# The first unit of K, loaded as eight transfers of every eighth partition, the first of them ahead of all weights

## The chip, the cores and the metric

The kernel runs on one core of a Trainium2 chip. The core has five engines that run their own instruction streams: TensorE (PE in the profile; PEld is its loading of weights), VectorE (DVE), ScalarE (ACT), GpSimd (POOL) and SyncE (SP), which here does nothing but issue transfers. Sixteen DMA engines carry data between HBM and the on-chip memory SBUF, which has 128 partitions. The metric is the device time of one execution in microseconds (us), as a median over runs.

## The reference

Two branches start from the same normalized input and are added to it. Branch A is one decoding step of attention with a cached window, branch B a small mixer and MLP. There are 4 sequences (B), one token each, width 576; attention has 32 query heads on 16 key/value heads (G = 16) of width 128, and the last 2048 of 8192 cached positions are read.

```python
def _A_ref(x, k_cache, v_cache, wq, wo):
    W = min(4096, max(256, Sk // 4))
    q = (x @ wq).reshape(B, Sq, Hq, Dh).transpose(0, 2, 1, 3)
    k = jnp.repeat(k_cache[:, :, Sk - W:, :], rep, axis=1)
    v = jnp.repeat(v_cache[:, :, Sk - W:, :], rep, axis=1)
    scores = jnp.einsum("bhqd,bhkd->bhqk", q, k) * (Dh ** -0.5)
    p = _softmax(scores, axis=-1)
    o = jnp.einsum("bhqk,bhkd->bhqd", p, v)
    return o.transpose(0, 2, 1, 3).reshape(B, Sq, Hq * Dh) @ wo

def _B_ref(x, w1, w2, w3, w4):
    h = _gelu(_layernorm(x, axis=-1) @ w1)
    ...
    x1 = x + hs
    return x1 + _gelu(_layernorm(x1, axis=-1) @ w3) @ w4

xn = _layernorm(A_x, axis=-1)
return A_x + _A_ref(xn, ...) + _B_ref(xn, ...)
```

With one token per sequence, the shifts of branch B (left out above) leave nothing of the shifted parts.

## The kernel before

The work is small in arithmetic and large in data: 88.5 MB of caches and weights pass through SBUF once. The kernel builds a list of operations for each engine. `add` (line 168) puts one on an engine's list with what it waits for, the signal that it gives and a key; `add_dma` (line 172) does the same for one or several transfers, which share a semaphore that grows by 16 for each. At the end every list is sorted by key (line 564), and that is the engine's program. So the order on SP's queue is the order of keys, and an operation that waits holds up all that stands behind it on its engine.

On SP's queue stand, in this order: `wq` in three transfers (keys -20, -18, -15; lines 221 to 223), W1 and W2 of branch B with two each (-14, -13), W3 in three (-12, -10, -8), then the units of K (keys 0 to 15) with the first unit of V between (key 8.5), then the rest of V, `wo` and W4 in five pieces. The small input x is issued by ScalarE at the very start.

A unit (`kv_pairs`, line 231) is one key/value head for all four sequences: 128 partitions of 16 KB, 2 MB in one transfer. Partition p = 4i + b holds 64 consecutive positions of sequence b, for i from 0 to 31. K's units go to a ring of four slots (`kring`), V's to another (`vring`), so from the fifth on a K unit waits for the last transposes of the unit four before it.

TensorE's order: the projections of the weights as they land, zeroing of the score accumulators (`pe_zeroS`, key -1, line 326), and then a loop of four rounds of four units. For each unit it transposes K in eight groups of eight blocks (`pe_T`, line 337), which DVE and ScalarE copy out of PSUM, and multiplies the transposed K with the queries (line 353). The first transposes of each unit wait for that unit's semaphore, ("k", slot), to reach 16 in each round. Then come the softmax, the products with V (line 434), `wo` and W4 (lines 449 and 531), and the output.

## Time and profile before

| | us |
|---|---|
| median of 3 runs | 215.08 |
| lowest and highest | 215.01, 215.12 |
| the profiled execution, device time | 215.35 |
| its span, first to last instruction | 214.0 |

| engine | busy us | share of the span |
|---|---|---|
| PE | 139.3 | 65% |
| PEld | 108.2 | 51% |
| DVE | 85.1 | 40% |
| ACT | 59.3 | 28% |
| POOL | 10.8 | 5% |

The profile page divides the span into 40 equal slices. A row of digits gives the busy share of an engine in each, in tenths; the row "DMA" the mean busy share of the 16 DMA engines, and "GB/s" what they moved. A row of the windows gives, for a stretch of time that begins the row, its length, the busy time and number of instructions of PE, PEld, DVE, ACT and POOL, then the clock granted to TensorE, the DMA share (1.00 is 16 engines busy) and GB/s; a packet is counted where it starts, so a short window can show a share above 1. Rows of queues give the packets that start in the window, their MB, and the time that they take as a share of 16 engines over the window. A row of the chain of waits gives start, duration, and what the end of the program hung on in that time. Rows of DMA packets count all and those under 512 B, which are almost all the 4-byte marks with which an engine reports its part of a transfer done.

### The profile page before, as it was taken

The page shows a single profiled execution, that of the slowest core. Times are in us where ns is not written, and L with a number is a line of the kernel's source. Part 1 is how long each engine was busy: PE and PEld are TensorE (multiplying, and loading weights), DVE is VectorE, ACT ScalarE, POOL GpSimd, SP SyncE. Part 2 cuts the span into 40 slices and gives each one's busy share as a digit, 9 for nine tenths or more (in the row PEclk, how much of TensorE's full clock was granted, in tenths as well). Part 3 has the DMA queues.
Part 4 walks back from the last instruction along what each step waited for, and adds up shares of the span by engine and source line. Part 5 has one row for each costly group of instructions (what it writes and reads, how often), then busy time and mean ns, then how long its engine had stood idle before and what let it go on. Part 6 is the DMA issues. An engine that isn't in the chain of part 4 may idle for free.

```text
span 214.0 us, 5789 instructions
## 1 busy us (share of the span) xinstructions
PE 139.3 (65%) x2670; PEld 108.2 (51%) x2672; DVE 85.1 (40%) x162; ACT 59.3 (28%) x72; POOL 10.8 (5%) x38
## 2 busy tenths in 40 slices
PE   0368375999999994999999719913344443333585
PEld 0114222877777883788887604813333443333444
DVE  5502602666666664466666569611111111100000
ACT  2001222466665553265666653000000000000000
POOL 8201000000000000000000000000000000000000
PEclk9999855899999999699999995555555555555579
DMA  7999999999999999999999999999999999999992
GB/s 243 426 398 447 441 405 435 416 424 426 432 423 429 429 432 426 429 429 430 426 429 429 432 429 441 423 423 426 426 432 429 423 429 426 429 432 425 428 408 108
DMA packets 6946, 88.63 MB, mean 414 GB/s; under 512 B 781, under 2 KB 1177, under 8 KB 1945
## 3 DMA queue, kind: packets, MB, share of 16 engines
q1 hardware_dynamic: 6920, 88.50, 97.7%
q8 instruction: 7, 0.11, 0.2%
q14 instruction: 3, 0.02, 0.0%
q10 hardware_dynamic: 16, 0.01, 0.0%
HBM read 88.49 MB, written 0.00 MB: 414 GB/s over the span
## 4 chain that ended last, share of the span: by engine, by line
DMA 52%; PE 36%; DVE 4%; SPq 4%; issue 2%; ACT 0%
DMA vring<-in_A_v_cache_dram 23%; PE ps L337 23%; DMA kring<-in_A_k_cache_dram 21%; DMA vring<-in_B_w_dram 8%; PE ps L353 7%; PE ps L434 4%; SPq L179 4%; PE ps L531 1%; DVE PTb L387 1%; DVE rmax L379 1%; DVE regB L345 1%; DVE PTs L395 1%; PE ps L410 0%; ACT P_sb L384 0%; DVE out_sb L558 0%
## 5 line engine op out<-in xcount | busy, mean ns | idle before, releaser
L345 DVE COPY regB<-ps 128x1024 bf16<-128x1024 bf16 x80 | 52.4, 687 | 34.3 <-PE ps L337 32.5
L337 PEld LDWEIGHTS ps<-perm_k,kring 128*128 128x128 bf16 x1024 | 58.9, 99 | 11.9 <-issue 8.6
L337 PE MATMUL ps<-perm_k,kring 128*128 128x128 bf16 x1024 | 62.2, 222 | 3.5 <-DMA kring<-in_A_k_cache_dram 3.5
L344 ACT ACTIVATE regB<-ps 128x1024 bf16<-128x1024 bf16 x48 | 47.6, 1022 | 41.1 <-PE ps L337 41.1
L434 PE MATMUL ps<-PTg,vring 128*128 128x8 bf16 x1024 | 29.5, 168 | 39.4 <-DMA vring<-in_A_v_cache_dram 37.0
L434 PEld LDWEIGHTS ps<-PTg,vring 128*128 128x128 bf16 x1024 | 28.4, 104 | 40.4 <-DMA vring<-in_A_v_cache_dram 27.5
L442 DVE TENSOR_TENSOR PTb<-ps,PTb 128x32 bf16<-128x32 f32 x16 | 3.1, 191 | 56.5 <-PE ps L434 56.5
L353 PE MATMUL ps<-regB,Qs 128*32 128x512 bf16 x272 | 18.8, 397 | 4.6 <-issue 3.5
L541 ACT ACTIVATE P_sb<-ps 100x288 f32<-100x288 f32 x1 | 0.4, 410 | 75.8 <-PE ps L449 75.8
L353 PEld LDWEIGHTS ps<-regB,Qs 128*32 128x32 bf16 x272 | 6.6, 97 | 10.8 <-issue 6.4
L398 DVE TENSOR_TENSOR PTg<-PTs,bmask 128x512 bf16<-128x512 bf16 x16 | 10.7, 681 | 0.0
L375 POOL COPY Qs<-Qpad 128x128 bf16<-128x128 bf16 x16 | 4.6, 293 | 92.6 <-PE ps L353 81.2
L515 PE MATMUL ps<-regB,x1nT 128*32 128x432 bf16 (+1 forms) x60 | 5.4, 520 | 1.9 <-DMA regB<-in_B_w_dram 1.4
L279 PE MATMUL ps<-ident_bf,xn_bf 4*128 4x4 bf16 x8 | 0.6, 170 | 8.8 <-DVE ragsrc L272 8.8
L301 PE MATMUL ps<-vring,xnT 128*32 128x512 bf16 x40 | 4.6, 629 | 2.1 <-DMA vring<-in_A_wq_dram 2.1
L388 PE MATMUL ps<-PTb,perm_p 128*128 128x512 bf16 x3 | 1.8, 609 | 4.9 <-DVE PTb L387 4.8
L279 PEld LDWEIGHTS ps<-ident_bf,xn_bf 4*128 4x128 bf16 x8 | 0.4, 112 | 8.8 <-POOL ones_f L215 6.3
L528 DVE STREAM_TRANSPOSE h2T_sb<-PTb 128x1152 bf16<-128x1152 bf16 x1 | 1.4, 1378 | 8.3 <-ACT PTb L525 8.3
L515 PEld LDWEIGHTS ps<-regB,x1nT 128*32 128x32 bf16 x60 | 2.0, 132 | 4.8 <-DMA regB<-in_B_w_dram 2.7
L558 DVE CAST out_sb<-ps 36x144 bf16<-36x144 f32 x1 | 0.3, 300 | 9.8 <-PE ps L531 9.8
L449 PE MATMUL ps<-kring,ORT 128*4 128x288 bf16 x64 | 3.8, 429 | 0.4 <-DVE ORT L463 0.4
L265 ACT ACTIVATE sd<-mv 4x1 f32<-4x1 f32 x3 | 0.6, 202 | 12.1 <-DVE mv L263 12.1
(98 smaller groups left out, 72.0 us busy)
## 6 DMA issues: line engine op xcount, KB each, us to landing
kring<-in_A_k_cache_dram SPq DMA_DIRECT2D x16, 2048.0 KB, 15.7
vring<-in_A_v_cache_dram SPq DMA_DIRECT2D x16, 2048.0 KB, 17.6
regB<-in_B_w_dram SPq DMA_DIRECT2D x2, 2304.0 KB, 21.5
kring<-in_A_wo_dram SPq DMA_DIRECT2D x1, 4608.0 KB, 24.0
vring<-in_A_wq_dram SPq DMA_DIRECT2D x2, 2048.0 KB, 9.8
vring<-in_B_w_dram SPq DMA_DIRECT2D x2, 2016.0 KB, 17.5
vring<-in_B_w_dram SPq DMA_DIRECT2D x2, 576.0 KB, 13.8
vring<-in_B_w_dram SPq DMA_DIRECT2D x1, 720.0 KB, 14.3
```

The costliest lines, as they stand in the source:

```text
L179: e.dma_start(o_, i_).then_inc(S[skey], 16)
L301: ins = e.matmul(Qps[32 * j:32 * j + 32, k, :], lhsT=x_, rhs=w, start=(r == 0), stop=(r == 4), tile_position=(0, 32 * j))
L337: ins = e.transpose(tb[n % NTB][:, t, :], kring[:, g % NKS, 8 * k + t, :], perm_k[:])
L344: return "act", lambda e: e.activation(out=ktbuf[:, n % NKT], in_=src, func=ACTF.Copy)
L345: return "dve", lambda e: e.tensor_copy(out=ktbuf[:, n % NKT], in_=src)
L353: ins = e.matmul(Sps[32 * b:32 * b + 32, c4, :].rearrange("p (t i) -> p t i", t=16), lhsT=Qs[:, g % 4, b, :], rhs=kttile[:, t0:t0 + 16, b, :],
L375: P(lambda e, g=g: e.tensor_copy(out=Qs[:, g % 4], in_=Qpad[:, g]), waits=(["qT"] if g == 0 else []) + ([f"SC{g - 4}"] if g >= 3 else []), ...
L398: add("dve", lambda e, g=g: e.tensor_tensor(out=PTg[:, g % NPG], in0=PTs[:, :, 2 * g:2 * g + 2].unsqueeze(2).to_broadcast([128, NT, B, 2]) ...
L434: ins = e.matmul(OTps(g), lhsT=vring[:, g % NVS, t, :], rhs=PTg[:, g % NPG, t].rearrange("p b e -> p (b e)"), start=(t == 0), stop=(t == N ...
L442: add("dve", lambda e, g=g: e.tensor_tensor(out=OTx[:, :, 2 * g:2 * g + 2, :], in0=OTps(g).rearrange("p (b e) -> p b e", b=B).unsqueeze(3) ...
L449: return e.matmul(ACC[h], lhsT=lhsT, rhs=rhs, start=start, stop=stop, tile_position=(k0, 32 * h))
L515: ins = e.matmul(H2ps[k][32 * j:32 * j + 32, :], lhsT=x_, rhs=w, start=(r == 0), stop=(r == 4), tile_position=(0, 32 * j))
```

## The change

The loop that issues the units of K begins with the second unit. The first is cut into eight transfers, named by s from 0 to 7. Transfer s takes the partitions s, s + 8, ..., s + 120, which are 16 partitions of 16 KB, 256 KB. Their source is sequence s mod 4 and, of the 32 stretches of positions, those with i = 2e + s // 4 for e from 0 to 15, so every partition gets the data that it had before. Transfer 0 has key -21 and stands ahead of `wq`, the first on SP's queue. Transfers 1 to 6 stand behind W3 (key -0.5), and transfer 7 (key 0) is the one that counts for the semaphore ("k", 0). Transfers 0 to 6 share a new semaphore, "comb"; TensorE waits for all seven behind the zeroing matmuls.

```diff
-        for g in range(G):
+        def comb(s_):
+            return (kring_t[s_:128:8, 0:UE],
+                    A_k_cache[s_ % B, 0, Sk - W:Sk, :].rearrange("(e j t) d -> e j (t d)", j=2, t=NT)[:, s_ // B, :])
+        add_dma([comb(0)], "comb", (), -21)
+        ev_comb = add_dma([comb(s_) for s_ in range(1, 7)], "comb", (), -0.5)
+        ev_k.append(add_dma([comb(7)], ("k", 0), (), 0))
+        add("pe", lambda e: None, [ev_comb], None, -0.5)
+        for g in range(1, G):
             ev_k.append(add_dma(kv_pairs(kring_t, g % NKS, A_k_cache, g), ("k", g % NKS),
                                 [f"T{8 * (g - NKS) + 7}"] if g >= NKS else [], g))
```

## The prediction

> **What bounds the kernel now.** I read the page from top to bottom first: the 40 slices, the queues, the chain by engine.

> ```profile
> span 214.0 us, 5789 instructions
> ...
> DMA  7999999999999999999999999999999999999992
> GB/s 243 426 398 447 441 405 435 416 424 426 432 423 429 429 432 426 429 429 430 426 429 429 432 429 441 423 423 426 426 432 429 423 429 426 429 432 425 428 408 108
> ...
> q1 hardware_dynamic: 6920, 88.50, 97.7%
> q8 instruction: 7, 0.11, 0.2%
> ```

> The 16 DMA engines are full in every slice but the first and the last two, and SP's queue (q1) carries nearly every byte. So the kernel is one stream of 88.5 MB. The windows give its speed, and how it runs out:

> ```profile
> 36.00:62.00 26.00, 24.60 (x400) 20.52 (x400) 15.70 (x25) 13.90 (x14) 1.47 (x5) 0.95 1.01 429
> 140.00:190.00 50.00, 18.10 (x621) 17.33 (x621) 7.29 (x19) 0.00 (x0) 0.00 (x0) 0.50 1.00 427
> 208.00:209.00 1.00, 0.25 (x5) 0.00 (x0) 0.00 (x0) 0.00 (x0) 0.00 (x0) 1.00 0.98 396
> 209.00:210.00 1.00, 0.97 (x32) 0.97 (x34) 0.00 (x0) 0.00 (x0) 0.00 (x0) 1.00 0.71 266
> 210.00:211.00 1.00, 1.00 (x40) 0.98 (x34) 0.00 (x0) 0.00 (x0) 0.00 (x0) 1.00 0.38 143
> 211.00:212.00 1.00, 1.00 (x32) 0.67 (x24) 0.00 (x0) 0.00 (x0) 0.00 (x0) 1.00 0.03 10
> ```

> 429 GB/s over 16 engines is 26.8 GB/s each, so a 16 KB packet (16384 B) takes 16384/26.8 = 0.611 us on its engine, and a unit of K or V (128 packets, 8 per engine) 4.89 us. The share of busy engines falls from 0.98 to 0.03 over some 2 us: the engines do not finish together, and the last one sets the end. The chain of waits says what hangs on the stream:

> ```profile
> 9.14 27.14 DMA kring<-in_A_k_cache_dram
> 36.28 0.13 issue
> 36.41 1.89 PE ps L337 x16
> ...
> 171.91 17.64 DMA vring<-in_A_v_cache_dram
> 189.55 0.05 issue
> 189.60 1.88 PE ps L434 x64
> 191.48 0.02 issue
> 191.50 17.49 DMA vring<-in_B_w_dram
> 208.99 0.04 issue
> 209.03 3.11 PE ps L531 x88
> 212.14 0.02 issue
> 212.17 0.30 DVE out_sb L558
> ```

> The V units come at the stream's pace: 17.64 + 0.05 + 1.88 + 0.02 = 19.59 us for four, 4.90 each against 4.89 of pure transfer, so the boundary between two queued transfers costs no more than about 0.01 us. The end is the landing of W4's second piece (208.99) plus 3.2 us of TensorE and DVE. Because SP's queue always holds work, **the time moves by just as much as the stream's slowest engine moves**. TensorE's long share in the K stage (L337) sits beside a full stream and buys nothing.

> **The change part by part.** *Bytes:* none are added; 256 KB of K's first unit move from behind W3 to the very front, and the other seven eighths stay at their place as seven transfers of 16 packets. *Semaphore marks:* seven more boundaries at up to 0.01 us, 0.07 us. *SP's issues:* seven more.

> ```profile
> 2.19 1.07 SPq L179 DMA_DIRECT2D vring<-in_B_w_dram  x2
> 5.42 3.68 SPq L179 DMA_DIRECT2D regB<-in_B_w_dram  x1
> 9.14 4.53 SPq L179 DMA_DIRECT2D kring<-in_A_k_cache_dram  x4
> ```

> Two issues take 1.07 us, so one is about 0.5, and seven add 3.7 us on SP; the 3.68 us of the third is SP held by a full queue, not by work. The first issue delays every weight issue by 0.5 us, the others come between W3 and K's second unit, which SP now has issued by 13.67 us and which the stream reaches after 36. That cover of over 20 us hides all of them; without it they would cost 3.7. *The new wait on PE* for the seven early eighths stands behind the zeroing matmuls and before the first transposes; behind it on PE is only T0, which waits for K's first unit anyhow. *Weights* land up to 0.61 us later; the first transposes today wait 0.45 us for K alone, so with an unmoved stream PE could start up to 0.2 us later. That moves SP's next K issues, which run far ahead: a K transfer lands 15.7 us after its issue, 4.89 of it its own. So nothing; without that lead, 0.2.

> ```profile
> 36.41 1.89 PE L337 MATMUL ps<-perm_k,kring 128*128 128x128 bf16 x16 [0.45 <-DMA kring<-in_A_k_cache_dram]
> ...
> kring<-in_A_k_cache_dram SPq DMA_DIRECT2D x16, 2048.0 KB, 15.7
> ```

> *The start.* I asked for the packets of the first microseconds by their starting times: 1.75 to 2.60, then 1.82 to 2.12, then 2.12 to 2.60.

> ```profile
> q1 hardware_dynamic: 16, 0.26, 147.3%
> ...
> q1 hardware_dynamic: 12, 0.20, 329.6%
> ...
> q1 hardware_dynamic: 4, 0.07, 54.8%
> ```

> The first packet of each engine takes 1.473 x 16 x 0.85 us / 16 = 1.25 us on average, twice the steady 0.611, and four engines start up to some 0.5 us after the other twelve. If the wait is for the 128 descriptors of the first transfer, 16 descriptors shorten it: the gain is at most the excess, 0.6 us. If it is the first reading itself, the gain is 0.

> *Where the eighths land.* The trace of before holds no transfer that touches every eighth partition. The nearest row is that of x, the only transfer to a few partitions early on: 4 packets of 1152 B into partitions 0 to 3, starting between 1.74 and 1.82. Beside it, W4's last packets of the same size, spread over 128 partitions, one engine still at work (211.04 to 211.34, seven of them and one mark).

> ```profile
> q10 hardware_dynamic: 4, 0.00, 30.9%
> ...
> q1 hardware_dynamic: 8, 0.01, 7.6%
> ```

> x: 0.309 x 16 x 80 ns / 4 = 99 ns for a packet. W4: 0.076 x 16 x 300 ns / 7 = 52 ns. Four packets under way at once into four neighbouring partitions take about twice as long each, as if those partitions stand behind one entry that carries about one engine's rate. It may instead be the slow start just shown; I think the entry likelier. On that reading the 32 groups of four stand, two by two, behind 16 entries, since 16 engines run at full rate together. A comb touches 16 groups, every other one. If an entry's two groups are neighbours, the comb has 16 entries and loses nothing; if they are 8, 16, 32 or 64 partitions apart, both are touched together and it has 8. By this count four of five pairings halve its rate: each 16 KB packet takes 1.22 us in place of 0.611.

> [...]

> **The size of that term.** Seven combs cost an engine 7 x 0.611 = 4.28 us if its partner runs abreast; combs 1 to 3 meet in one set of entries and 4 to 7 in the other, so a pair whose leader is L ahead loses L less in each set, 4.28 - 2L. How far apart are they? The marks with which the engines end K's first unit tell: the packets of 34.0 to 34.8 and of 35.4 to 36.2 (those under 512 B are marks), and below them the packet of the instruction queue that starts at 29.36, by a window of 20 ns:

> ```profile
> DMA packets 32, 0.28 MB, mean 348 GB/s; under 512 B 15, under 2 KB 15, under 8 KB 15
> ...
> DMA packets 28, 0.44 MB, mean 553 GB/s; under 512 B 1, under 2 KB 1, under 8 KB 1
> ...
> q8 instruction: 1, 0.02, 335.9%
> ```

> Fifteen engines mark the unit's end within 0.8 us, one about 1.5 us later: most likely the one that fetched instructions (3.359 x 16 x 20 ns = 1.07 us, and its data beside it). For the fifteen L is a few tenths; with L = 0.15 they lose 4.0. The late one loses 4.28 - 2 x 1.5 = 1.3 and is no longer last. So K's first unit lands 4.0 - 1.4 = 2.6 us later (36.28 to about 38.9). By the end there have been seven fetches, on several engines, and the last engine is some 2.1 us behind the first (the shares from 209 on); a fetch on one of the shifted engines gives 4.0 + 0.2 + 1.5 - 2.1 = 3.6. Bounds 2.6 and 4.3; I take 3.6. For the first comb: from -0.6 (start shortened, no sharing) to +0.61 (shared); under sharing I take +0.3, as a shorter start gives back half. Sum: 3.6 + 0.3 + 0.07 = 4.0 us. The profiled execution took 215.35 us (its span 214.0 and 1.35 around it), 0.27 above the median 215.08; so 219.3 for it, **219.1 for the median**. Own range: from 2.6 - 0.6 to 4.3 + 0.61 + 0.07, 217.1 to 220.1.

> **The rivals.** *Not slower, no sharing, start unchanged:* x's 99 ns are only the slow beginning, the combs run at 0.611 a packet, and the first 16 packets pay the same 1.25 us whichever they are: 215.08 + 0.07, 215.1. For it: all 16 engines are slow then, not x alone. Against: a start that adds 0.64 us to the other packets would hardly leave x's done in 0.1 us. *Faster:* no sharing, and the first wave starts at once: four late engines gain 0.5 and the stream with them: 215.08 - 0.5 = 214.6. For it: 16 descriptors against 128; against: the late engines are not all last, and the weights' own 128 descriptors still follow 0.5 us later. *Sharing that sorts itself:* one engine of a pair is served first and runs away by L near 1.5, as the late one does today; the loss falls to 1.3 and with the start to +1.5, 216.6. For it: the late engine's row; against: no reason for an uneven service. *The change does not do what it says:* the 16 packets of a comb go to 8 engines, two each; that too is 1.22 us a comb, and with fewer engines 2.4 or more: beyond 223.

> **How the numbers follow.** Chances: forecast 0.62, self-sorting 0.13, no change 0.13, faster 0.09, beyond 0.03. This kernel's measurement tells about 0.2% (0.43 us) from no change; so faster 0.09, same 0.13, slower 0.62 + 0.13 + 0.03 = 0.78. The range 215.0 to 220.1 takes in the forecast, self-sorting and most of no change, and leaves out the faster case and the tails, some 2 in 10.

> **What would show it.** Right: a window over the seven combs (about 30 to 38 us) at 215 to 300 GB/s, not 429, with packets of 1.0 to 1.25 us; the first K transposes start near 39 us; SP and PE waits unchanged in kind; later windows again at 429; the end later by about 4 us. Wrong: that window at 420 or more, and the first transposes at 36.4 or before. The first comb's packets tell the start: near 0.6 us each is a gain, 1.25 none, 1.8 sharing on top.

## The result and the profile after

| | median us | lowest, highest | runs |
|---|---|---|---|
| before | 215.02 | 214.91, 215.12 | 6 |
| changed | 220.90 | 220.14, 222.25 | 6 |

The ratio is 1.0275, with a 95% interval of 1.026 to 1.0291: 5.9 us slower, where 4.0 was forecast with an own range up to 220.1. The scatter is new as well: 0.2 us before, over 2 us after. The profiled execution is the slowest of the six, 222.25 us, so its numbers are set against the 215.35 of the profiled execution before: +6.9. In the tables below, runs over 1.5% above the fastest of the same kernel are left out of the ratio, though not of the median: 223.15 us of e11_before_w1, and 224.52 and 635.8 us of e6_by_batch.

From the page of the changed kernel, the slices and the queues:

```profile
span 221.0 us, 5798 instructions
...
DMA  6999999999999999999999999999999999999991
GB/s 214 430 400 445 427 316 206 347 427 420 427 424 427 427 427 427 430 427 429 430 433 427 430 449 454 401 407 433 430 427 427 421 430 427 427 427 428 426 384 47
...
q1 hardware_dynamic: 7032, 88.50, 97.1%
q8 instruction: 7, 0.11, 0.2%
```

The DMA engines are as busy as before and move the same 88.50 MB. But in slices 6 to 8 (28 to 44 us) the rate falls to 316, 206 and 347 GB/s; elsewhere, but for the first slice and the last two, it is 400 or more. Engines that are as busy at half the rate take twice as long for each packet. The windows over this stretch of the changed kernel, with the DMA share and GB/s last:

```profile
31.00:32.00 1.00, 0.34 (x7) 0.14 (x10) 0.00 (x0) 0.00 (x0) 0.00 (x0) 0.50 1.20 222
32.00:33.00 1.00, 1.00 (x20) 0.53 (x16) 0.00 (x0) 0.00 (x0) 0.00 (x0) 0.50 1.02 206
33.00:34.00 1.00, 0.77 (x12) 0.12 (x4) 0.00 (x0) 0.00 (x0) 0.00 (x0) 0.50 1.00 189
34.00:35.00 1.00, 0.00 (x0) 0.00 (x0) 0.00 (x0) 0.00 (x0) 0.00 (x0) 0.50 0.85 180
...
44.00:62.00 18.00, 17.28 (x265) 13.67 (x262) 10.59 (x16) 9.79 (x10) 0.88 (x3) 0.89 1.01 426
```

At 180 to 222 GB/s with a share near 1, all 16 engines hold a packet and each gets half of its 26.8 GB/s. The packets that start between 31 and 39 us in the changed kernel, all of them and then SP's queue:

```profile
DMA packets 204, 1.65 MB, mean 206 GB/s; under 512 B 99, under 2 KB 99, under 8 KB 105
...
q1 hardware_dynamic: 204, 1.65, 101.5%
```

1.015 x 16 x 8 us is 130 us of packet time; less about 4 us for the 99 marks and 6 small packets, 126 us for 99 packets of 16 KB, 1.27 us each against 0.611. From 44 us on the stream is back at 426 GB/s. The chain of waits of the changed kernel shows nearly the whole delay when K's first unit lands:

```profile
14.70 28.18 DMA kring<-in_A_k_cache_dram
42.88 0.13 issue
43.01 1.89 PE ps L344 x16
...
198.51 17.47 DMA vring<-in_B_w_dram
215.98 0.04 issue
216.03 3.11 PE ps L538 x88
```

That landing moved from 36.28 to 42.88, by 6.6 us, and the last landing on the chain from 208.99 to 215.98, by 7.0. So 0.4 us are added between the two; what lies behind is as long as before (3.11 us for the last matmuls in both).

### The profile page after: what moved, and what is told of

It reads as the page before. It is cut to its first block, busy times and chain, and to the rows that moved or that the text cites. A ratio compares the mean times of both kernels' runs of the same rounds, so it can differ in the third digit from the quotient of the medians.

```text
span 221.0 us, 5798 instructions
## 1 busy us (share of the span) xinstructions
PE 137.8 (62%) x2672; PEld 107.0 (48%) x2672; DVE 85.1 (39%) x162; ACT 59.6 (27%) x72; POOL 10.8 (5%) x38
## 3 DMA queue, kind: packets, MB, share of 16 engines
q1 hardware_dynamic: 7032, 88.50, 97.1%
## 4 chain that ended last, share of the span: by engine, by line
DMA 50%; PE 35%; SPq 6%; DVE 4%; issue 3%; ACT 0%
PE ps L344 22%; DMA vring<-in_A_v_cache_dram 22%; DMA kring<-in_A_k_cache_dram 20%; DMA vring<-in_B_w_dram 8%; PE ps L360 7%; SPq L179 6%; PE ps L441 4%; PE ps L538 1%; DVE PTb L394 1%; DVE rmax L386 1%; DVE regB L352 1%; DVE PTs L402 1%; PE ps L417 0%; ACT P_sb L391 0%; DVE out_sb L565 0%
## 5 line engine op out<-in xcount | busy, mean ns | idle before, releaser
L352 DVE COPY regB<-ps 128x1024 bf16<-128x1024 bf16 x80 | 52.4, 687 | 34.8 <-PE ps L344 33.2
L395 PE MATMUL ps<-PTb,perm_p 128*128 128x512 bf16 x4 | 2.4, 608 | 4.3 <-DVE PTb L394 4.1
L532 ACT ACTIVATE PTb<-ps 128x432 bf16<-128x432 f32 (+1 forms) x3 | 1.3, 491 | 10.6 <-PE ps L522 10.6
L538 PE MATMUL ps<-vring,h2T_sb 128*4 128x144 bf16 x88 | 3.1, 226 | 1.2 <-DMA vring<-in_B_w_dram 1.2
## 6 DMA issues: line engine op xcount, KB each, us to landing
vring<-in_A_v_cache_dram SPq DMA_DIRECT2D x16, 2048.0 KB, 17.6
kring<-in_A_k_cache_dram SPq DMA_DIRECT2D x15, 2048.0 KB, 14.7
vring<-in_A_wq_dram SPq DMA_DIRECT2D x2, 2048.0 KB, 9.8
```

What stands on the lines that cost most here:

```text
L352: return "dve", lambda e: e.tensor_copy(out=ktbuf[:, n % NKT], in_=src)
L538: return e.matmul(FIN[h][z], lhsT=lhsT, rhs=rhs, start=start, stop=stop, tile_position=(0, 32 * h))
```

## The experiments

Medians in us; the kernel before, timed beside each group, gave 215.01 to 215.07. Edits that take lines out are shown against the changed kernel, those with added lines alone against the kernel before; there the shorter loop over K and the added wait of TensorE are as in the change and left out.

| run | median | lowest, highest | ratio, 95% interval |
|---|---|---|---|
| e1_late8 | 220.90 | 220.17, 221.44 | 1.0267, 1.024 to 1.0294 |
| e2_free8 | 217.23 | 217.16, 217.35 | 1.0103, 1.0086 to 1.012 |
| e3_block16 | 227.17 | 226.88, 227.91 | 1.0575, 1.0553 to 1.0598 |
| e4_early2k | 216.75 | 216.64, 216.88 | 1.0078, 1.0061 to 1.0095 |
| e5_before_w3 | 219.97 | 219.77, 222.06 | 1.026, 1.0208 to 1.0312 |
| e6_by_batch | see there | | |
| e7_half64 | 220.55 | 219.91, 221.02 | 1.0263, 1.0241 to 1.0286 |
| e8_stride7 | 219.43 | 219.12, 219.66 | 1.0202, 1.0185 to 1.0219 |
| e9_early_batch | 215.07 | 214.92, 215.25 | 1.0005, 0.9996 to 1.0015 |
| e10_block32 | 220.72 | 220.67, 222.62 | 1.0294, 1.0256 to 1.0332 |
| e11_before_w1 | 221.27 | 219.66, 223.15 | 1.0279, 1.0234 to 1.0325 |
| e12_changed_again | 221.12 | 220.10, 223.29 | 1.0267, 1.0252 to 1.0282 |

**All eight late.** The early place alone undone:

```diff
-        add_dma([comb(0)], "comb", (), -21)
-        ev_comb = add_dma([comb(s_) for s_ in range(1, 7)], "comb", (), -0.5)
+        ev_comb = add_dma([comb(s_) for s_ in range(7)], "comb", (), -0.5)
```

> All eight eighths behind W3, the weights first as before: only the early place of the first is undone. Shared entries (partitions 8 apart reach 8 of 16 entries, a packet takes about 1.24 us): eight combs lose 8 x 0.63 = 5.0 us on engines that run abreast, and the late engine adds up to 1: 220 to 221.2, packets of 1.2 us between 30 and 40 us. Rival, the early first transfer is what costs: near 215.1 with the combs at 0.61 us a packet.

220.90, the same as the changed kernel. The early place is not what costs. A row of its windows gives 213 GB/s over five microseconds of combs, 262144 B in 1.23 us where 0.611 would do:

```profile
32.00:37.00 5.00, 3.04 (x16) 0.73 (x16) 1.38 (x1) 1.26 (x3) 0.00 (x0) 0.50 0.99 213
```

**The same places, all partitions.** Eight transfers of 256 KB as in the change, each an eighth of the bytes of all 128 partitions.

```diff
+        def part(s_):
+            o_, i_ = kv_pairs(kring_t, 0, A_k_cache, 0)[0]
+            return (o_[:, 1024 * s_:1024 * (s_ + 1)], i_[:, :, 1024 * s_:1024 * (s_ + 1)])
+        add_dma([part(0)], "comb", (), -21)
+        ev_comb = add_dma([part(s_) for s_ in range(1, 7)], "comb", (), -0.5)
+        ev_k.append(add_dma([part(7)], ("k", 0), (), 0))
```

> The same eight transfers of 256 KB at the same eight places as in the changed kernel, but each has all 128 partitions and an eighth of their bytes (2 KB). Shared entries: no loss from meeting; 2 KB packets cost about 0.06 us per transfer and engine more (from 93 ns for 2304 B in the trace of before), and the start up to 0.4: 215.1 to 216.0. Rival, a fixed cost of every small transfer (0.6 us each): 219 to 221, as in the changed kernel.

217.23: above the range for shared entries, below the rival's. Eight small transfers as such do not cost 5.9 us. Where its own 2.2 come from, the next run but one tells.

**Blocks of 16 neighbours.**

```diff
-            return (kring_t[s_:128:8, 0:UE],
+            return (kring_t[16 * s_:16 * s_ + 16, 0:UE],
```

with all eight late, as in the first run.

> As with all eight behind W3, but transfer s fills the 16 neighbouring partitions from 16s on, so K's first unit stands on other partitions. Shared entries: 16 neighbours are four groups behind four entries, four engines each, so a packet takes 2.4 us and the eight lose 8 x 1.83 = 14.6 us: 227 to 232. Rival, the cost is that of one packet per engine and transfer, whatever the partitions: the same as with the combs, 220 to 221.

227.17, 12.15 slower. The same sources, sizes and number of transfers, other partitions, and twice the loss: the destination sets the price, not the reading and not the transfer. Two windows of it, the first over the same five microseconds as above:

```profile
32.00:37.00 5.00, 1.73 (x20) 0.29 (x12) 0.00 (x0) 0.65 (x2) 0.00 (x0) 0.50 1.13 149
33.00:36.00 3.00, 0.85 (x12) 0.29 (x12) 0.00 (x0) 0.00 (x0) 0.00 (x0) 0.50 0.96 127
```

Neither is as low as the quarter (107) that four entries would give; the four were my estimate, for groups of one entry 16 or more partitions apart. Why is not shown; engines that run ahead into the next block, behind other entries, would do it.

**The start alone, in 2 KB packets.**

```diff
+        o_, i_ = kv_pairs(kring_t, 0, A_k_cache, 0)[0]
+        ev_comb = add_dma([(o_[:, 0:1024], i_[:, :, 0:1024])], "comb", (), -21)
+        ev_k.append(add_dma([(o_[:, 1024:UE], i_[:, :, 1024:UE])], ("k", 0), (), 0))
```

> Only the start: one transfer of 256 KB ahead of all weights that fills 2 KB of all 128 partitions, and the other 14 KB of each in one transfer behind W3. Shared entries: nothing is shared, so what is left is the early start alone: between -0.5 and +0.5, 214.6 to 215.5. Rival, the early transfer carries much of the loss: 216 or more.

216.75, above the expected range and where the rival put it: 1.7 us from one early transfer of 128 partitions. So most of the second run's 2.2 us was its start, and its six further transfers cost 217.23 - 216.75 = 0.48. The windows of the first microseconds, in the kernel before, the changed kernel and this one:

```profile
2.00:5.00 3.00, 0.00 (x0) 0.00 (x0) 2.67 (x6) 0.87 (x2) 3.00 (x6) 1.00 0.83 306
```

```profile
2.00:5.00 3.00, 0.00 (x0) 0.00 (x0) 2.67 (x6) 0.87 (x2) 3.00 (x6) 1.00 1.00 333
```

```profile
2.00:5.00 3.00, 0.00 (x0) 0.00 (x0) 2.67 (x6) 0.86 (x2) 3.00 (x6) 1.00 0.88 189
```

Here the short packets are slow while the stream starts (189 GB/s with the engines 0.88 busy, against 306 with 0.83 before); why was not tried. For the question here this run is spoilt by its packets, and the start was measured again below.

**Every fourth partition.** Four transfers of 32 partitions, one sequence each, all late.

```diff
+        def comb(b_):
+            return (kring_t[b_:128:4, 0:UE], A_k_cache[b_, 0, Sk - W:Sk, :].rearrange("(i t) d -> i (t d)", t=NT))
+        ev_comb = add_dma([comb(b_) for b_ in range(3)], "comb", (), -0.5)
+        ev_k.append(add_dma([comb(3)], ("k", 0), (), 0))
```

> K's first unit behind W3 in four transfers of 32 partitions, every fourth one, so each transfer reaches all 32 groups of four and gives an engine two packets. What counts is which packets are under way at one time: engines begin with partitions 8e + b, half of the entries, and go on with 8e + 4 + b, the other half: half rate, 219.5 to 221. Rival, what counts is how many entries the transfer reaches in all: no loss, 215.0 to 215.4.

Its four runs gave 214.97, 215.19, 224.52 and 635.8; what made the last two so long is not known, and there is no ratio. The profile is that of the run of 215.19 (span 213.8), and its window is clear:

```profile
32.00:37.00 5.00, 1.77 (x12) 1.05 (x13) 1.38 (x1) 1.12 (x3) 0.00 (x0) 0.84 1.00 426
```

Full rate: no loss, and the rival was right. On the reading by entries, these transfers reach all of them and their engines do not meet, although 32 packets are only two for each engine.

**Halves, blocks of 32, every seventh partition.** Three ways to ask how, on the reading of the prediction, an entry's two groups of four partitions lie.

```diff
+        ev_comb = add_dma([(o_[0:64], i_[0:16])], "comb", (), -0.5)
+        ev_k.append(add_dma([(o_[64:128], i_[16:32])], ("k", 0), (), 0))
```

> K's first unit behind W3 in two transfers, partitions 0 to 63 and 64 to 127. If an entry's two groups lie 32 partitions apart, each half reaches 8 entries and runs at half rate: 219.5 to 221. If they lie 64 apart, each half reaches 16 groups on 16 entries: no loss, 215.0 to 215.4.

220.55. Half rate (213 GB/s, where every fourth partition had 426), so by that reading the two groups of an entry do not lie 64 partitions apart. The block of 32 is the run with every fourth partition, the same four transfers of the same data, with `kring_t[32 * b_:32 * b_ + 32, 0:UE]` as destination:

> K's first unit behind W3 in four transfers of 32 neighbouring partitions (0 to 31 and so on; the unit stands on other partitions). Groups of an entry 32 partitions apart: each transfer reaches 8 entries, a packet takes 1.22 us, 219.5 to 221. Groups 8 or 16 apart, which the combs and the halves of 64 leave possible: 4 entries, 2.4 us a packet, 226 to 230. If 32 partitions are spread over 16 entries in any way, as with every fourth one: 215.0 to 215.4.

220.72: half rate (216 GB/s) and not a quarter (107), so they do not lie 8 or 16 apart either. The window of each, first the halves, then the blocks of 32:

```profile
32.00:37.00 5.00, 2.65 (x16) 0.54 (x8) 1.38 (x1) 1.25 (x3) 0.00 (x0) 0.50 0.99 213
```

```profile
32.00:37.00 5.00, 1.04 (x4) 0.31 (x4) 1.38 (x1) 1.18 (x3) 0.00 (x0) 0.84 1.02 216
```

With the combs (213 GB/s) against 4, only 32 is left of the five pairings that the prediction counted. This chooses among the five; the groups of four and the 16 entries are supposed in it and not shown. The third way:

```diff
-            return (kring_t[s_:128:8, 0:UE],
+            return (kring_t[s_:s_ + 106:7, 0:UE] if s_ < 7 else kring_t[112:128, 0:UE],
```

> Eight transfers of 16 packets behind W3 as in the run with all eight late, but seven of them take every seventh partition (s, s + 7, ..., s + 105), the eighth the 16 neighbours from 112 on; K's first unit stands on other partitions. Counted out for entries whose groups lie 32 apart, only 24 of the 112 packets of the seven meet another (at most three on one engine): worst engine 1.2 to 1.8 us, and 1.5 us for the block of 16 (an eighth of the 12.15 us of the run with blocks): 217.0 to 218.6. For entries 64 or 8 apart, five or six of seven packets of an engine meet: 219.5 to 220.5. Rival, every 16-packet transfer is slow: 220.9.

219.43, between the two expectations and in neither. Its window, 272 GB/s, lies between half and full rate:

```profile
32.00:37.00 5.00, 1.04 (x4) 0.31 (x4) 1.38 (x1) 1.05 (x3) 0.00 (x0) 0.84 1.13 272
```

The direction is that of the pairing by 32, the size is not. My count held only if engines stay abreast. That a packet which meets another makes its engine late, so that it meets those of the next transfer too, would explain the rest, but no run shows it.

**The start alone, without sharing.** The four transfers of every fourth partition, the first of them ahead of the weights (`add_dma([comb(0)], "comb", (), -21)`).

> Only the start, in packets of 16 KB and at full rate: K's first unit in four transfers of every fourth partition, which ran at 0.615 us a packet when all stood behind W3; now the first of them (512 KB) stands ahead of all weights. In the changed kernel the first packets started at 2.2 us, not 1.83, behind an issue of 0.62 us, not 0.41: so the early transfer costs 0.2 to 0.6, 215.2 to 215.6. Rival, a short first transfer gains once nothing is shared: 214.4 to 214.8.

215.07, ratio 1.0005: neither a cost nor a gain, and outside both expected ranges. The window of its first microseconds shows more started than in the three above,

```profile
2.00:5.00 3.00, 0.00 (x0) 0.00 (x0) 2.67 (x6) 0.86 (x2) 3.00 (x6) 1.00 0.98 360
```

but the marks of the first weights (16 per transfer: SP's queue has 7032 packets in the changed kernel against 6920, 112 more for seven more transfers; the trace has the time at which each arrives, though not from which engine) come 1.17 us later than before on the last engine (9.54 against 8.37), and 512 KB take 1.22 us at 429 GB/s: 0.05 gained. This kernel also has three of SP's seven additional issues and PE's additional wait. They cost nothing.

**Where the combs stand.** The remaining question was the engine that comes late into the combs.

```diff
-        ev_comb = add_dma([comb(s_) for s_ in range(1, 7)], "comb", (), -0.5)
-        ev_k.append(add_dma([comb(7)], ("k", 0), (), 0))
+        ev_comb = add_dma([comb(s_) for s_ in range(1, 7)], "comb", (), -12.6)
+        ev_k.append(add_dma([comb(7)], ("k", 0), (), -12.5))
```

> The seven later eighths move ahead of W3, where in the trace of before all engines end a transfer within 0.5 us and none has yet fetched instructions beside it. The late engine held up by the combs of the others: without one there, the median engine loses the same 4.5 us over the combs, but the last engine is no further behind at K's second unit than before the change (1.5 us behind the median, not 2.5), and the time is 219.9 to 220.5, with less scatter than the changed kernel. Rival, the late engine does not matter: the same 220.9 with the same scatter of 2 us. PE starts K some 3 us later than in the changed kernel, since W3 lands later; SP's lead covers that.

219.97, in the range, but one of four runs gave 222.06, so the scatter did not go. The other place uses keys -14.6 and -14.5, timed beside the changed kernel:

> The seven later eighths a step earlier still, between the query weights and W1: again no engine is late when the combs run. Late engine held up by the combs of the others: 219.7 to 220.3, as with the combs ahead of W3 (219.97), and at least 0.6 under the changed kernel timed beside it. Rival, the place does not matter: within 0.3 of the changed kernel.

> The changed kernel once more, on the same chip as the run with the combs ahead of W1, so that the two stand side by side: 220.5 to 221.3 by its earlier runs, with a scatter of about 2 us.

The combs ahead of W1 gave 219.66, 219.88 and 220.18 in three runs, 222.36 to 223.15 in the others; the changed kernel 220.10 to 223.29. The ratios, 1.0279 and 1.0267, do not tell the two apart. Without the run of 223.15 the medians are 220.18 and 221.12, but three low and two high runs settle nothing: the expected 0.6 is not shown. The marks say a little more. At K's second unit the last engine lies 1.5 us behind the median in the run with the combs ahead of W3 (45.997 against 44.475) and 1.6 with the combs ahead of W1, as before the change (41.166 against 39.657, 1.5), but 2.5 in the changed kernel (47.53 against 45.07) and 3.3 in its second profile (49.27 against 45.93). These two profiles are of the longest runs of the changed kernel, though, the other two of short ones; and with all eight late (221.08), where one engine also comes late into the combs (2.6 us behind at W3's last piece), it is 1.7.

## Why the prediction was wrong

**The bound** was right: the stream is full, and the time moved with its slowest engine. **SP's issues and PE's wait** at nothing: right as far as tested. The start without sharing has the wait and three of the issues and costs nothing; the run of 2 KB parts has all seven issues and took only 0.48 us more than the one with a single additional issue, its six further short transfers included. What held SP for 3.68 us at one issue, which the prediction puts to a full queue, no run shows. **The start:** in itself it is worth 0.0 (e9_early_batch), not a gain. The changed kernel's first packets, those starting between 2.1 and 2.7 us, take 1.617 x 16 x 0.6 / 16 = 0.97 us:

```profile
q1 hardware_dynamic: 16, 0.26, 161.7%
```

They and the weights behind them let the first weights' marks come 1.04 us later in the median (8.99 against 7.96) for 0.61 us of data: the first comb costs 0.4, where 0.3 was taken. Its own packets do not show sharing: in e9_early_batch, where nothing is shared, the same window gives 0.94 us. The sixteen packets after them take 0.90 us in the changed kernel, less a little for 16 marks, and 0.63 in e9_early_batch (3.1 to 3.7 and 2.9 to 3.5 us):

```profile
q1 hardware_dynamic: 32, 0.26, 150.3%
```

```profile
q1 hardware_dynamic: 16, 0.26, 105.0%
```

```profile
q10 hardware_dynamic: 3, 0.00, 20.2%
```

Of the signs named, the window over the combs came out lower (206 GB/s against 215 to 300) and the packets longer (1.27 us against 1.0 to 1.25), and the first transposes started at 43.0 us, not near 39; from 44 on the stream was full again (426 GB/s), as forecast.

**What failed is the size of that term**, at "For the fifteen L is a few tenths; with L = 0.15 they lose 4.0. The late one loses 4.28 - 2 x 1.5 = 1.3 and is no longer last." Two things are wrong in it. First, leads gave nothing: in the run with all eight late the combs took 9.94 us between the median marks of W3's last piece and K's first unit (29.97 and 39.91), 1.24 each, so seven lose 7 x (1.24 - 0.61) = 4.4. Second, the late engine lost more than the others, not less. In the changed kernel the fetch of instructions comes earlier, at 28.43 (first row below, a window of 20 ns, 1.07 us as before). By the times at which one packet ends and the next begins, its engine then still has nine packets of W3 to write, eight of them of 4608 B between 30.67 and 34.30, while the others begin the combs at 30.24. In the kernel before the fetch starts at 29.36, and that engine's mark for W3 follows at its end (30.42). So the late engine entered the stretch still writing W3, as I read it to an entry which two engines were filling with combs. One of its 4608 B packets starts at 33.23 (second row, 20 ns), the last packet of this kind in the kernel before at 29.63 (third row, 10 ns); beside the first, a comb's packet that starts at 33.37 (last row, 10 ns):

```profile
q8 instruction: 1, 0.02, 333.8%
```

```profile
q1 hardware_dynamic: 1, 0.00, 170.6%
```

```profile
q1 hardware_dynamic: 1, 0.00, 116.2%
```

```profile
q1 hardware_dynamic: 1, 0.02, 1118.1%
```

1.706 x 16 x 20 ns is 546 ns, 1.162 x 16 x 10 ns is 186 ns: three times as long. And 11.181 x 16 x 10 ns is 1.79 us, three times 0.611, as for an entry shared by three; in that stretch four packets of combs take 1.72 to 1.83 us, the others between 31 and 36 us at most 1.47. (I infer the sharing from the times; the trace does not name destinations.) The late engine's mark for W3's last piece comes at 35.86, 4.8 us behind the median engine's 31.06; in the kernel before it was 1.7 behind (31.52 against 29.87). So K's first unit landed at 42.88 and not at 38.9, and the late engine was the last still.

The sum, remade: 4.4 for seven combs and 0.4 for the first are 4.8. The run with the combs ahead of W3, where no engine comes late into them, bears that out: at K's second unit its median engine is 4.8 us later than before (44.475 against 39.657), and its profiled time is 219.84. The lowest runs of the changed kernel (220.10 and 220.14) are 5.1 above before. What single runs lose beyond that is in part the last engine's lag and in part a further delay of the median engine. In the profile of 222.25 us the median mark of W4's second piece is 5.8 us later than before (213.11 against 207.34), and the last engine's lag there has grown from 1.65 to 2.87; in the one of 223.29 the median mark is 7.4 us later (214.71) and the lag 2.3. In that second profile the late engine was already 1.8 us late at the first weights (10.85 against 9.09) and 5.4 at W3's last piece. How a late engine holds up the others, and what sets apart a run that has one from a run without, stays open, as do the high runs of the combs ahead of W1, of which there is no profile.

**The rivals:** no sharing (215.1) and the faster start (214.6) fell with the result; the start without sharing shows that 215.1 was right for a first transfer that shares nothing. Sharing that sorts itself: the late engine lost more than the others, not less. That the packets go to eight engines: no, the share of busy engines stays near 1 while the rate halves (0.99 at 213 GB/s in e1_late8).

## What to carry to other kernels

Before a transfer is cut by partitions, ask which partitions its packets fill at one time: here every eighth partition (213 GB/s), 64 neighbours (213) or 32 neighbours (216) ran at half rate, every fourth partition (426) or all 128 (429) at full rate, for the same bytes and packets. A stretch in which the DMA engines are busy (share 0.99) and the rate is half was the sign of it. In a stream that all the rest waits for, price the engine that comes last, and do not let it profit from being late unless a row shows that.

## What the runs showed of the hardware

Unexpected were three things. One engine falls some 1.5 us behind the others, which by the times alone I put to a fetch of instructions (a packet of 16 KB, 1.07 us, at 29.36 in the kernel before); there the last mark lies 1.4 to 2.0 us behind the median from K's first unit to the last piece of W4. 256 KB in packets of 2 KB ahead of the first weights cost 1.7 us (e4_early2k), while 512 KB in packets of 16 KB to every fourth partition cost 0.05 or less (e9_early_batch). And transfers to 32 partitions each ran at 426 GB/s with every fourth one (e6_by_batch), but at 216 with neighbours (e10_block32).
